# Top-32 attention and a gated MLP on one core: the first MLP layer on two token blocks at once

## The chip, the cores and the metric

The kernel runs on one core of a Trainium2 chip. The metric is the device time of one execution in microseconds. An execution of the kernel before takes 1560.32 us, the median of three runs.

## What is computed

Eight batches of eight heads are attended to, 576 tokens of 64 dimensions each. Of every row of scores only the 32 largest survive. The result goes through a two-layer MLP with a quick-GELU gate between.

```python
scores = (q @ k.T) / sqrt(64)                  # 8 batches, 8 heads, 576 x 576
kth    = 32nd largest of each row
p      = exp(where(scores >= kth, scores, -1e9) - rowmax)
attn   = (p / (p.sum(-1) + 1e-9)) @ v
x      = attn laid out as 4608 tokens x 512    # heads side by side
h      = x @ w_in                              # 512 -> 2048
g      = h / (1 + exp(-1.702 * h))
out    = g @ w_out                             # 2048 -> 512
```

All data are float32.

## The kernel before

**Slots and rounds.** The attention is cut into 144 slots, 18 for each batch. A slot is 128 query rows of one pair of heads. The first four full blocks of a batch (`t` = 0 to 3) have four slots each, one for each pair of heads. Two further slots hold the 64-row ends of two pairs of heads each, and they come between blocks 2 and 3. The first 12 slots are run one by one by `slot(n)`, with a plain search for the 32 largest, while the weights are loaded and rounded. All later ones are run two at a time by `two_slots(n)`, here called a round: 66 rounds find the largest of slots 12 to 143, and two more finish what is left. The order of the work within a round is written out by hand and holds for each engine's queue.

**What a round does.** In each half of a round, VectorE finds the largest of a slot (`topk_of_pairs`, begun by `pair_up`, line 322), GpSimd forms the lesser of each pair (lines 325 and 326), and ScalarE makes the exponentials (lines 387 and 390) and splits them (line 461) so that a DMA can transpose them by way of DRAM (lines 463 and 469). TensorE computes scores for two later slots (line 281), the attention output of two earlier slots (`values_at`, line 526), and two groups of each MLP layer. ScalarE copies scores out of PSUM (line 293).

**The MLP.** `x_of` (line 544, GpSimd) writes a slot's 128 columns of x into a tile `xT` of one block of 128 tokens. Where the last pair of heads of a block is in, `finish_x` puts the tile on the list `ready`. `hidden` (line 575) takes the first tile of the list and computes four of the sixteen slices of 128 hidden units, for the 128 tokens: 16 matmuls of 128 columns, which fill one PSUM bank. This is called a group here; a block has four. `tanh` (ScalarE, lines 592 and 595) and `gate` (GpSimd, lines 604 and 605; VectorE, line 607, at the end) turn the group into the gated activation, and `project` (line 622) multiplies it with `w_out`, four matmuls of 512 columns, into a PSUM bank `po` that collects the sixteen slices of a block. After the fourth group `leave` copies `po` out (line 628) and stores it. The 64-row ends of two batches make one further block of 128 tokens in a tile of their own (`xT_t`). That makes 36 blocks and 144 groups.

**Where a group can be computed.** A round calls `hidden` twice, once before the attention output of the round and once behind `x_of`, and `project` twice. Where `ready` is empty, the call does nothing. After the last round `last_slot` is repeated until all groups are done.

**Buffers.** There are two tiles `xT` (`xtp`), so the first `x_of` of a block waits until the groups of the block before the last are computed. In the rounds, the first `hidden` of a round writes into the bank `ps_h` and the second into the two-bank pool `ps_t`. Tiles for raw q and k (`loads`) are double, those for v (`vals`) sixfold. The tables READY, FETCH and VALUES say, for the four pairs of heads of a batch, how many slots before or after the batch's first slot they are prepared, loaded, and their v is loaded; READY_1 and FETCH_1 are those of the second batch.

Of the kernel before, what the change touches and what calls it, by code (L numbers as in the profile page):

```python
# [9 lines left out]
ALU = mybir.AluOpType  # L10
# [20 lines left out]
def kernel(  # L31
# [57 lines left out]
    const = ctx.enter_context(tc.tile_pool(name="const", bufs=1))  # L89
    pool = lambda name, bufs, **kw: ctx.enter_context(tc.tile_pool(name=name, bufs=bufs, **kw))  # L90
    raws = pool("raws", 8)
    loads = pool("loads", 2)
    vals = pool("vals", 6)
    qkt = pool("qkt", 6)
    scp = pool("scp", 4)
    prp = pool("prp", 2)
    lefts = pool("lefts", 2)
    small = pool("small", 4)
    ptp = pool("ptp", 2)
    xtp = pool("xtp", 2)  # L100
    xtt = pool("xtt", 1)
    thp = pool("thp", 5)
    apart = pool("apart", 4, space=DRAM)
# [54 lines left out]

    qT, kT, vv = {}, {}, {}
    loaded = {}  # L160
    v_ends = [const.tile([P, 2, D], F32, name=f"v_e{i}") for i in range(6)]
    for i, t in enumerate(v_ends):
        (nc.gpsimd if i else nc.vector).memset(t[:], 0.0)

# [6 lines left out]
    def load(name, b, hp, queue=None):  # L171

        src = q if name == "q" else k
        if (b, hp) not in loaded:
            loaded[b, hp] = loads.tile([P, 2 * NF + 1, 2, D], F32, name="qk_l")
        t = loaded[b, hp]
        if queue is None:
            heads_of = lambda j: of_load(name, t)[:, :, j, :]
        else:
            heads_of = lambda j: heads_apart(name, t)[:, j, :, :]  # L180
        queue = queue or nc.sync
        for j in range(2):
            queue.dma_start(heads_of(j), src[b, 2 * hp + j, 0:FULL, :].rearrange("(p t) d -> p t d", t=NF))

        on = slice(0, TAIL) if name == "q" else slice(TAIL, P)
        queue.dma_start(t[on, 2 * NF, :, :], src[b, 2 * hp : 2 * hp + 2, FULL:S, :].rearrange("h p d -> p h d"))
# [283 lines left out]

    xts = {}

    def values(n, put_off=None):

        b, t, hps = slots[n]
        pt = st[n]["pt"]
        outs = []
        for p in range(2 if t == NF else 1):
            cols = slice(p * TAIL, (p + 1) * TAIL) if t == NF else slice(0, P)
            main, tail = vv[b, hps[p]]  # L480
            o = ps_t.tile([P, 512], F32, name="o", tag="tp")
            for c in range(NF + 1):
                for j in range(2):
                    nc.tensor.matmul(
                        o[j * D : (j + 1) * D, 0 : cols.stop - cols.start],
                        lhsT=main[:, j, c, :] if c < NF else tail[:, j, :],
                        rhs=pt[:, MAIN[j] + c if c < NF else NF, cols],
                        start=(c == 0),
                        stop=(c == NF),
                    )  # L490
            outs.append((o, hps[p]))
        st[n].clear()

        def bring():
            for o, hp in outs:
                if t < NF:
                    if (b, t) not in xts:
                        xts[b, t] = xtp.tile([P, CC, P], F32, name="xT")
                    nc.scalar.copy(out=xts[b, t][:, hp, :], in_=o[:, 0:P])
                else:  # L500
                    if (b // 2, t) not in xts:
                        xts[b // 2, t] = xtt.tile([P, CC, P], F32, name="xT_t")
                    at = b % 2 * TAIL
                    nc.scalar.copy(out=xts[b // 2, t][:, hp, at : at + TAIL], in_=o[:, 0:TAIL])
            finish_x(n)

        if put_off is None:
            bring()
        else:
            put_off.append(bring)  # L510
# [24 lines left out]
    def x_of(m, o, by):  # L535

        b, t, hps = slots[m]
        for p in range(2 if t == NF else 1):
            cols = slice(p * TAIL, (p + 1) * TAIL) if t == NF else slice(0, P)
            key, tile_of = ((b // 2, t), xtt) if t == NF else ((b, t), xtp)  # L540
            if key not in xts:
                xts[key] = tile_of.tile([P, CC, P], F32, name="xT_t" if t == NF else "xT")
            to = slice(b % 2 * TAIL, (b % 2 + 1) * TAIL) if t == NF else cols
            nc.gpsimd.tensor_tensor(  # L544
                out=xts[key][:, hps[p], to], in0=o[:, cols], in1=by[:, cols], op=ALU.mult
            )
        finish_x(m)

    def finish_x(m):

        b, t, hps = slots[m]
        if hps[-1] == NP - 1:
            if t < NF:
                to = out[b * S : b * S + FULL, :].rearrange("(p t) c -> p t c", t=NF)[:, t, :]
                ready.append((xts.pop((b, t)), [(slice(0, P), to)]))
            elif b % 2:
                first = [(b - 1 + i) * S + FULL for i in range(2)]
                rows = [(slice(i * TAIL, (i + 1) * TAIL), out[x : x + TAIL, :]) for i, x in enumerate(first)]
                ready.append((xts.pop((b // 2, t)), rows))

    ready = []
    hidden_at = {"g": 0}
    to_gate, gated, to_project = [], [], []
    proj = {}

    def hidden(into=None):
        if not ready:
            return
        xT, rows = ready[0]
        g = hidden_at["g"]  # L570
        ph = (into or ps_h).tile([P, G, P], F32, name="ph", tag="tp" if into else "ph")
        for i in range(G):
            f = g * G + i
            for c in range(CC):
                nc.tensor.matmul(  # L575
                    ph[:, i, :],
                    lhsT=win[:, c, f * P : (f + 1) * P],
                    rhs=xT[:, c, :],
                    start=(c == 0),
                    stop=(c == CC - 1),  # L580
                )
        to_gate.append((ph, g, rows))
        hidden_at["g"] = (g + 1) % NG
        if g == NG - 1:
            ready.pop(0)

    def tanh(aside):

        if to_gate:
            ph, g, rows = to_gate.pop(0)  # L590
            th = thp.tile([P, G, P], F32, name="th")
            nc.scalar.activation(th[:], ph[:], AF.Tanh, scale=0.851 / RAISE)  # L592
            if aside:
                h = raws.tile([P, G, P], F32, name="h", tag="raw")
                nc.scalar.copy(out=h[:], in_=ph[:])
                ph = h
            gated.append((th, ph, g, rows))

    def gate(aside):
        if not gated:  # L600
            return
        th, h, g, rows = gated.pop(0)
        if aside:
            nc.gpsimd.tensor_scalar(th[:], th[:], 1.0, 1.0, op0=ALU.add, op1=ALU.mult)
            nc.gpsimd.tensor_tensor(out=th[:], in0=th[:], in1=h[:], op=ALU.mult)  # L605
        else:
            nc.vector.scalar_tensor_tensor(  # L607
                out=th[:], in0=th[:], scalar=1.0, in1=h[:], op0=ALU.add, op1=ALU.mult
            )
        to_project.append((th, g, rows))  # L610

    def project(blocks, put_off_leaving=False):

        if blocks[0] == 0:
            proj["on"] = to_project.pop(0)
            if proj["on"][1] == 0:
                proj["po"] = ps_p.tile([P, C], F32, name="po")
        gT, g, rows = proj["on"]
        po = proj["po"]
        for i in blocks:  # L620
            f = g * G + i
            nc.tensor.matmul(  # L622
                po[:], lhsT=gT[:, i, :], rhs=wout[:, f, :], start=(f == 0), stop=(f == FC - 1)
            )
        if blocks[-1] == G - 1 and g == NG - 1:
            def leave():
                ob = thp.tile([P, C], F32, name="ob", tag="th")
                nc.scalar.mul(out=ob[:], in_=po[:], mul=0.5 / RAISE**2)
                for on, to in rows:
                    nc.sync.dma_start(to, ob[on, :])  # L630

            leaving.append(leave)
            if not put_off_leaving:
                leave_all()

# [13 lines left out]


    READY = (-12, -10, -4, -2)
    READY_1 = (-6, -4, -3, -2)
    FETCH = (-16, -14, -8, -6)
    FETCH_1 = (-12, -10, -5, -3)
    VALUES = (-2, -1, 1, 2)
    by_slot = dict(enumerate([2, 2, 3, 3, 3, 3, 3, 3, 3, 3, 2, 2]))
    for n in by_slot:
        first = sum(map(len, list(by_slot.values())[:n]))
# [21 lines left out]

    def may_project(waiting):

        return len(to_project) > waiting and len(finished) >= NG * CC + (to_project[0][1] + 1) * G

    def both_heads(to, src, t):

# [67 lines left out]
    def slot(n):  # L754
# [65 lines left out]
            for fn, args in preparing:  # L820
                fn(*args)
        if n > PROJECTS and may_project(2):
            project(range(G))
        if idle:
            stay_warm(8)
        hidden()
# [1 line left out]
    def last_slot():  # L828

        tanh(False)  # L830
        gate(False)
        if may_project(0):
            project(range(G))
        hidden()

    def two_slots(n):

# [21 lines left out]

        def project_one():  # L860
            if may_project(0):
                project(range(G), True)

        def measure(m):
            if live(m):
# [7 lines left out]
            split(n - 1)  # L873
        bring_all()
        find(n)
        hidden()
        project_one()
        tanh(aside)
        prepare_some(first)
# [76 lines left out]
```

## Time and profile before

| | us |
|---|---|
| median of three runs | 1560.32 |
| lowest and highest | 1559.6 and 1564.83 |
| the profiled execution | 1561.79 |
| its span, first to last instruction | 1560.0 |

The profile shows one execution on the chip. TensorE is busy 94% of the span and VectorE 88%; the mean granted clock of TensorE is 0.972 of full speed. A float32 matmul of the program stands as two records in the trace, so a group of the first layer is 32 records of 128 columns and a group of the second 8 records of 512.

### The profile page before, as it was taken

To read this page: it belongs to the slowest core of one execution; us is meant where nothing else is said; L and a number is where in the kernel's file an instruction comes from. 1 tells how busy PE (TensorE), PEld (TensorE's weight loads), DVE (VectorE), ACT (ScalarE), POOL (GpSimd) and SP (SyncE) were. 2 spreads that over 40 slices of the span, in tenths; PEclk is the share of its full clock that TensorE was granted. 3 is DMA by queue.
4 is the path that set the end of the run, shared out by engine and by line. 5 is a ranking of instruction groups with operands and counts; after the bars stand their busy time and mean duration, and the time that the engine had idled before them with its cause. 6 is when DMAs were issued, how large, how long until landed. Compare 5 with 4: busy or idle time off the path is not lost. (4 is left out here: it accounts for less than half of the span.)

```text
span 1560.0 us, 31382 instructions
## 1 busy us (share of the span) xinstructions
PE 1461.0 (94%) x10729; PEld 1059.6 (68%) x10729; DVE 1375.2 (88%) x4542; ACT 1171.5 (75%) x1846; POOL 888.9 (57%) x1119
## 2 busy tenths in 40 slices
PE   7789789999999899999998899999998899999997
PEld 5667556777766577777776577777775677777765
DVE  7999989999989799999997799999997889999700
ACT  6998778888768687878786687888876688777710
POOL 3788555666645566666665466666664566666400
PEclk8899899999999999999999999999999999999999
DMA  7451786767755486677767576676765658444500
GB/s 241 134 160 36 194 214 184 194 172 183 189 156 162 126 199 173 173 176 181 187 162 161 128 186 190 163 189 175 179 172 146 161 147 203 131 128 130 145 23 14
DMA packets 533778, 248.35 MB, mean 159 GB/s; under 512 B 465136, under 2 KB 507889, under 8 KB 533617
## 3 DMA queue, kind: packets, MB, share of 16 engines
q1 hardware_dynamic: 533184, 246.05, 60.3%
q8 instruction: 84, 1.38, 0.4%
q14 instruction: 78, 0.63, 0.1%
q10 hardware_dynamic: 432, 0.30, 0.1%
HBM read 45.09 MB, written 105.32 MB: 96 GB/s over the span
## 5 line engine op out<-in xcount | busy, mean ns | idle before, releaser
L622 PE MATMUL po<-wout,th 128*128 128x512 f32 x1152 | 534.2, 608 | 43.9 <-POOL th L605 35.4
L575 PEld LDWEIGHTS ph<-xT,win 128*128 128x128 f32 x4096 | 473.9, 192 | 69.6 <-issue 53.2
L575 PE MATMUL ph<-xT,win 128*128 128x128 f32 x4096 | 489.3, 277 | 12.3 <-POOL xT L544 12.3
L622 PEld LDWEIGHTS po<-wout,th 128*128 128x128 f32 x1152 | 213.5, 195 | 264.5 <-issue 216.4
L336 DVE MAX8 top<-left 128x8 f32<-128x288 f32 x792 | 325.3, 445 | 0.0
L461 ACT COPY sc<-pr 128x2304 uint16<-128x2304 uint16 x133 | 281.5, 2117 | 2.2
L293 ACT ACTIVATE sc<-s_ps 128x576 f32<-128x576 f32 x288 | 172.2, 654 | 140.6 <-PE s_ps L281 130.3
L544 POOL TENSOR_TENSOR xT<-x 128x128 f32<-128x128 f32 x117 | 51.7, 458 | 392.6 <-DVE top L343 215.1
L390 ACT ACTIVATE pr<-sc,low 128x576 f32<-128x576 f32 x288 | 220.6, 774 | 47.7 <-POOL low L367 47.7
L336 DVE MAX8 top<-lesser 128x8 f32<-128x288 f32 x528 | 214.1, 446 | 37.1 <-POOL lesser L326 37.1
L339 DVE MATCH_REPLACE8 left<-top,left 128x288 f32<-128x288 f32 x528 | 229.6, 442 | 0.0
L387 ACT ACTIVATE sc<-sc,cut 128x576 f32<-128x576 f32 x288 | 208.7, 783 | 2.7 <-POOL cut L378 2.1
L326 POOL TENSOR_TENSOR lesser<-lesser,greater 128x576 int32<-128x576 int32 x132 | 186.0, 1409 | 22.7 <-DVE greater L322 13.2
L325 POOL TENSOR_TENSOR lesser<-sc 128x576 int32<-128x576 int32 x132 | 187.6, 1421 | 0.0
L281 PE MATMUL s_ps<-qk_t 64*128 64x288 f32 (+1 forms) x1280 | 185.2, 436 | 1.0 <-ACT sc L293 0.8
L605 POOL TENSOR_TENSOR th<-th,h 128x512 f32<-128x512 f32 x127 | 161.9, 1275 | 10.6
L526 PE MATMUL o<-pt,v_l 128*64 128x128 f32 (+1 forms) x2384 | 147.5, 268 | 11.0 <-DMA pt<-rows 11.0
L526 PEld LDWEIGHTS o<-pt,v_l 128*64 128x64 f32 x2384 | 122.7, 139 | 38.1 <-issue 22.9
L592 ACT ACTIVATE th<-ph 128x512 f32<-128x512 f32 x144 | 86.6, 602 | 81.0 <-PE ph L575 80.9
L322 DVE TENSOR_TENSOR greater<-sc 128x576 f32<-128x576 f32 x132 | 104.6, 792 | 44.7 <-ACT sc L293 35.4
L281 PEld LDWEIGHTS s_ps<-qk_t 64*128 64x128 f32 (+1 forms) x1280 | 100.8, 180 | 42.6 <-issue 22.1
L339 DVE MATCH_REPLACE8 left<-top,greater 128x288 f32<-128x288 f32 x264 | 114.8, 442 | 0.0
(86 smaller groups left out, 1606.2 us busy)
## 6 DMA issues: line engine op xcount, KB each, us to landing
rows<-sc SPq DMA_DIRECT2D x133, 576.0 KB, 3.1
qk_rows<-halves SPq DMA_DIRECT2D x56, 256.0 KB, 2.8
qk_l<-in_q_dram SPq DMA_DIRECT2D x64, 128.0 KB, 3.0
raw<-in_moe_w_in_dram SPq DMA_DIRECT2D x16, 512.0 KB, 5.2
v_l<-in_v_dram SPq DMA_DIRECT2D x32, 256.0 KB, 3.2
raw<-in_moe_w_out_dram SPq DMA_DIRECT2D x16, 512.0 KB, 3.6
out_dram<-ob SPq DMA_DIRECT2D x32, 256.0 KB, 2.9
qk_l<-in_k_dram SPq DMA_DIRECT2D x62, 128.0 KB, 2.9
```

The source lines that it names most:

```text
L281: nc.tensor.matmul(ps[i][rows, c, 0:HALF], lhsT=qT[b, hps[p]][on, cols], rhs=kT[b, hps[p]][on, FIRST[i] + c * HALF : FIRST[i] + (c + 1) * ...
L293: nc.scalar.mul(out=to, in_=ps[i][:, :, 0:HALF], mul=SCALE)
L325: nc.gpsimd.tensor_tensor(out=whole, in0=a.bitcast(I32), in1=b.bitcast(I32), op=ALU.add)
L326: nc.gpsimd.tensor_tensor(out=whole, in0=whole, in1=greater[n][:].bitcast(I32), op=ALU.subtract)
L336: nc.vector.max(top[:, i, 8 * r : 8 * r + 8], src[:, i, :])
L339: nc.vector.match_replace(to[:, i, :], top[:, i, 8 * r : 8 * r + 8], src[:, i, :], LOWEST)
L387: nc.scalar.activation(sc[:, i, :], sc[:, i, :], AF.Prelu, bias=cut[:, i : i + 1], alpha=HUGE)
L390: nc.scalar.activation(pr[:, i * S : (i + 1) * S], sc[:, i, :], AF.Exp, bias=low[:, i : i + 1], accum_out=den[:, i : i + 1],)
L461: nc.scalar.copy(out=halves, in_=pr[:].bitcast(U16).rearrange("p (k h) -> p h k", h=2))
L526: nc.tensor.matmul(o[j * D : (j + 1) * D, cols], lhsT=main[:, j, c, :] if c < NF else tail[:, j, :], rhs=pt[:, MAIN[j] + c if c < NF else ...
L575: nc.tensor.matmul(ph[:, i, :], lhsT=win[:, c, f * P : (f + 1) * P], rhs=xT[:, c, :], start=(c == 0), stop=(c == CC - 1),)
L622: nc.tensor.matmul(po[:], lhsT=gT[:, i, :], rhs=wout[:, f, :], start=(f == 0), stop=(f == FC - 1))
```

## The change

A block pair replaces the block in the first layer. From the third block of the first batch on, the tile `xT` holds two blocks (`x_at` finds the place in it), it goes on the list `ready` when the second of them is finished, and a matmul of `hidden` has 256 columns. A group is then two slices of hidden units for 256 tokens, and still fills one PSUM bank; a block pair has eight groups. `project` has two accumulators for a block pair, one in `ps_p` and one in `ps_h`, and the number of its matmuls in a group stays four. In the rounds and in `last_slot`, every `hidden` writes into `ps_t`. Blocks 0 and 1 of the first batch and the blocks of ends stay single.

`xtp` has three tiles, each of two blocks. To make room there is one tile for raw q and k and four for v; the first batch's second and fourth pairs of heads use the tiles of `ptp` as load buffers. The tables of loads move to fit. `last_slot` calls `hidden` ahead of `gate` and `project`.

```diff
-    loads = pool("loads", 2)
-    vals = pool("vals", 6)
+    loads = pool("loads", 1)
+    vals = pool("vals", 4)
-    xtp = pool("xtp", 2)
+    xtp = pool("xtp", 3)
...
-            loaded[b, hp] = loads.tile([P, 2 * NF + 1, 2, D], F32, name="qk_l")
+            home, tag = (ptp, "pt") if b == 0 and hp % 2 else (loads, "qk_l")
+            loaded[b, hp] = home.tile([P, 2 * NF + 1, 2, D], F32, name="qk_l", tag=tag)
...
+    def x_at(b, t, hp):
+        if t < NF:
+            if (b, t // 2) not in xts:
+                xts[b, t // 2] = xtp.tile([P, CC, 2, P], F32, name="xT")
+            return xts[b, t // 2][:, hp, t % 2, :]
+        if b // 2 not in xts:
+            xts[b // 2] = xtt.tile([P, CC, P], F32, name="xT_t")
+        return xts[b // 2][:, hp, b % 2 * TAIL : (b % 2 + 1) * TAIL]
...
     def finish_x(m):
...
+        if b == 0 and t < 2:
+            ready.append(([xT[:, c, t, :] for c in range(CC)], [rows(t)]))
+        elif t % 2:
+            ready.append(([xT[:, c, :, :].rearrange("p w q -> p (w q)") for c in range(CC)], [rows(t - 1), rows(t)]))
...
     def hidden(into=None):
...
+        tiles = len(rows)
+        f0 = hidden_at["f"]
+        fs = range(f0, f0 + G // tiles)
+        ph = (into or ps_h).tile([P, G * P], F32, name="ph", tag="tp" if into else "ph")
+        for i, f in enumerate(fs):
             for c in range(CC):
                 nc.tensor.matmul(
-                    ph[:, i, :],
+                    ph[:, i * tiles * P : (i + 1) * tiles * P],
                     lhsT=win[:, c, f * P : (f + 1) * P],
-                    rhs=xT[:, c, :],
+                    rhs=xT[c],
...
+    def project(put_off_leaving=False):
+        gT, fs, rows = to_project.pop(0)
+        if fs.start == 0:
+            pos[:] = [
+                home.tile([P, C], F32, name="po", tag=tag) for home, tag in ((ps_p, "po"), (ps_h, "ph"))[: len(rows)]
+            ]
+        blocks = iter(range(G))
+        for f in fs:
+            for po in pos:
+                i = next(blocks)
+                nc.tensor.matmul(
+                    po[:], lhsT=gT[:, i * P : (i + 1) * P], rhs=wout[:, f, :], start=(f == 0), stop=(f == FC - 1)
+                )
...
-    READY_1 = (-6, -4, -3, -2)
-    FETCH = (-16, -14, -8, -6)
-    FETCH_1 = (-12, -10, -5, -3)
-    VALUES = (-2, -1, 1, 2)
+    READY_1 = (-7, -4, -3, -2)
+    FETCH = (-16, -11, -8, -3)
+    FETCH_1 = (-12, -6, -3, -2)
+    VALUES = (-1, 1, 1, 3)
...
     def last_slot():
         tanh(False)
+        hidden(ps_t)
         gate(False)
         if may_project(0):
-            project(range(G))
-        hidden()
+            project()
...
         find(n)
-        hidden()
+        hidden(ps_t)
         project_one()
```

## Rows read from the trace of the kernel before

**Rows 1.** The page's first part: engine, busy us, share of the span, instructions.

```profile
PE 1461.0 (94%) x10729; PEld 1059.6 (68%) x10729; DVE 1375.2 (88%) x4542; ACT 1171.5 (75%) x1846; POOL 888.9 (57%) x1119
```

**Rows 2.** Stretches: start:end, length, engines' busy us (instructions), granted clock, DMA share, GB/s.

```profile
145.68:241.72 96.04, 80.28 (x536) 53.34 (x532) 90.90 (x309) 75.89 (x112) 52.05 (x65) 0.91 0.72 185
460.59:525.18 64.59, 52.95 (x368) 36.56 (x368) 46.02 (x160) 37.73 (x58) 34.50 (x44) 0.89 0.50 134
825.42:890.31 64.89, 53.24 (x368) 36.61 (x368) 46.03 (x160) 37.73 (x58) 34.50 (x44) 0.89 0.55 143
1190.55:1255.51 64.96, 53.31 (x368) 36.60 (x368) 46.02 (x159) 37.73 (x58) 34.48 (x44) 0.89 0.55 139
1106.89:1164.21 57.32, 57.32 (x416) 41.79 (x415) 56.09 (x193) 44.30 (x71) 36.27 (x46) 1.00 0.73 178
1505.84:1560.00 54.16, 43.23 (x216) 28.53 (x215) 4.12 (x6) 4.78 (x8) 0.00 (x0) 0.99 0.04 10
```

**Rows 3.** The chain that ended last, one round: start, us, engine, line.

```profile
1121.10 0.22 PE o L515 x2
1121.32 1.17 PE s_ps L281 x8
1122.49 2.33 PE o L526 x40
1124.83 1.17 PE s_ps L281 x8
1126.00 3.77 PE ph L575 x32
1129.77 3.44 PE po L622 x8
1133.20 3.57 PE ph L575 x32
1136.77 3.44 PE po L622 x8
1140.21 0.22 PE o L515 x2
```

**Rows 4.** VectorE's order of time, the first instruction of three slots [idle before].

```profile
1123.82 0.76 DVE L322 TENSOR_TENSOR greater<-sc 128x576 f32<-128x576 f32 x1
1133.15 0.76 DVE L322 TENSOR_TENSOR greater<-sc 128x576 f32<-128x576 f32 x1
1142.92 0.76 DVE L322 TENSOR_TENSOR greater<-sc 128x576 f32<-128x576 f32 x1 [0.17 <-ACT sc L293]
```

**Rows 5.** Waits of the span: who for whom, us in total, times, longest.

```profile
POOL xT L544 <- PE ph L575: 55.4, 6, 9.2
DVE top L336 <- POOL lesser L326: 37.1, 6, 6.2
PE ph L575 <- POOL xT L544: 12.3, 16, 1.1
```

**Rows 6.** Order of time in one stall (1190 to 1200 us).

```profile
1190.36 3.73 PE L575 MATMUL ph<-xT,win 128*128 128x128 f32 x32
1194.17 0.45 POOL L544 TENSOR_TENSOR xT<-x 128x128 f32<-128x128 f32 x1 [9.22 <-PE ph L575]
1197.48 0.82 DVE L336 MAX8 top<-lesser 128x8 f32<-128x288 f32 x2 [6.18 <-POOL lesser L326]
```

**Rows 7.** Stretches: a wait of TensorE in the round of slots 18 and 19, and after.

```profile
217.00:224.98 7.98, 2.01 (x29) 1.33 (x25) 6.39 (x22) 4.03 (x8) 0.00 (x0) 0.76 0.71 223
224.98:227.50 2.52, 2.52 (x22) 2.19 (x24) 2.52 (x11) 0.07 (x1) 0.00 (x0) 0.50 0.02 6
```

**Rows 8.** The chain after the last round, one repetition and the last matmuls.

```profile
1512.71 3.58 PE ph L575 x32
1516.32 0.61 ACT th L592
1516.95 0.70 DVE th L607
1517.69 3.70 PE po L622 x8
...
1552.41 3.71 PE po L622 x8
```

**Rows 9.** Waits of the DMA queue (SP): who for whom, us in total, times, longest.

```profile
SPq L469 <- DMA rows<-sc: 292.8, 106, 4.5
SPq L469 <- PE s_ps L281: 145.1, 53, 7.0
```

More of the change, by code (lines that the diff above doesn't have):

```diff
@@ L160 @@
     loaded = {}
-    v_ends = [const.tile([P, 2, D], F32, name=f"v_e{i}") for i in range(6)]
+    v_ends = [const.tile([P, 2, D], F32, name=f"v_e{i}") for i in range(NP)]
     for i, t in enumerate(v_ends):
@@ L495, in bring @@
             for o, hp in outs:
[L496 to L504, printed above, removed]
+                to = x_at(b, t, hp)
+                nc.scalar.copy(out=to, in_=o[:, 0 : to.shape[-1]])
             finish_x(n)
@@ L539, in x_of @@
             cols = slice(p * TAIL, (p + 1) * TAIL) if t == NF else slice(0, P)
[L540 to L546, printed above, removed]
+            nc.gpsimd.tensor_tensor(out=x_at(b, t, hps[p]), in0=o[:, cols], in1=by[:, cols], op=ALU.mult)
         finish_x(m)
@@ L551, in finish_x @@
         b, t, hps = slots[m]
[L552 to L556, printed above, removed]
+        if hps[-1] < NP - 1:
+            return
+        if t == NF:
+            if b % 2:
                 first = [(b - 1 + i) * S + FULL for i in range(2)]
                 rows = [(slice(i * TAIL, (i + 1) * TAIL), out[x : x + TAIL, :]) for i, x in enumerate(first)]
-                ready.append((xts.pop((b // 2, t)), rows))
+                xT = xts.pop(b // 2)
+                ready.append(([xT[:, c, :] for c in range(CC)], [rows]))
+            return
+        lines = out[b * S : b * S + FULL, :].rearrange("(p t) c -> p t c", t=NF)
+        rows = lambda t: [(slice(0, P), lines[:, t, :])]
+        xT = xts[b, t // 2]
+        if b == 0 and t < 2:
+            ready.append(([xT[:, c, t, :] for c in range(CC)], [rows(t)]))
+        elif t % 2:
+            ready.append(([xT[:, c, :, :].rearrange("p w q -> p (w q)") for c in range(CC)], [rows(t - 1), rows(t)]))
+        if t % 2:
+            del xts[b, t // 2]
     ready = []
-    hidden_at = {"g": 0}
+    hidden_at = {"f": 0}
     to_gate, gated, to_project = [], [], []
-    proj = {}
+    pos = []
     def hidden(into=None):
@@ L569, in hidden @@
         xT, rows = ready[0]
[L570 to L573, printed above, removed]
+        tiles = len(rows)
[3 more added lines that the diff above has]
+        for i, f in enumerate(fs):
             for c in range(CC):
                 nc.tensor.matmul(
-                    ph[:, i, :],
+                    ph[:, i * tiles * P : (i + 1) * tiles * P],
                     lhsT=win[:, c, f * P : (f + 1) * P],
-                    rhs=xT[:, c, :],
+                    rhs=xT[c],
                     start=(c == 0),
@@ L581, in hidden @@
                 )
-        to_gate.append((ph, g, rows))
-        hidden_at["g"] = (g + 1) % NG
-        if g == NG - 1:
+        to_gate.append((ph, fs, rows))
+        hidden_at["f"] = fs.stop % FC
+        if fs.stop == FC:
             ready.pop(0)
@@ L590, in tanh @@
             ph, g, rows = to_gate.pop(0)
-            th = thp.tile([P, G, P], F32, name="th")
+            th = thp.tile([P, G * P], F32, name="th")
             nc.scalar.activation(th[:], ph[:], AF.Tanh, scale=0.851 / RAISE)
             if aside:
-                h = raws.tile([P, G, P], F32, name="h", tag="raw")
+                h = raws.tile([P, G * P], F32, name="h", tag="raw")
                 nc.scalar.copy(out=h[:], in_=ph[:])
@@ L610, in gate, with leave @@
         to_project.append((th, g, rows))
[L612 to L626, printed above, removed]
+    def project(put_off_leaving=False):
[11 more added lines that the diff above has]
+                )
+        if fs.stop == FC:
+            def leave(po, to_rows):
                 ob = thp.tile([P, C], F32, name="ob", tag="th")
                 nc.scalar.mul(out=ob[:], in_=po[:], mul=0.5 / RAISE**2)
-                for on, to in rows:
+                for on, to in to_rows:
                     nc.sync.dma_start(to, ob[on, :])
-            leaving.append(leave)
+            leaving.extend(lambda po=po, to=to: leave(po, to) for po, to in zip(pos, rows))
             if not put_off_leaving:
@@ L681, in may_project @@
     def may_project(waiting):
-        return len(to_project) > waiting and len(finished) >= NG * CC + (to_project[0][1] + 1) * G
+        return len(to_project) > waiting and len(finished) >= NG * CC + to_project[0][1].stop
     def both_heads(to, src, t):
@@ L830, in last_slot @@
         tanh(False)
+        hidden(ps_t)
         gate(False)
         if may_project(0):
-            project(range(G))
-        hidden()
+            project()
     def two_slots(n):
@@ L861, in project_one @@
             if may_project(0):
-                project(range(G), True)
+                project(True)
         def measure(m):
```

## The prediction

> **What bounds the kernel now.** I read the engines' shares first. TensorE is busy 94% of the span and VectorE 88% [rows 1], so neither alone explains 1560 us, and the stages have to be taken apart. The next view is the table of stretches [rows 2]. In an undisturbed one, three rounds from 1106.89 to 1164.21, TensorE is busy all 57.32 us and VectorE 56.09. The chain shows one such round [rows 3]: from 1121.10 to 1140.21 is 19.11 us, and TensorE's pieces lie end to end in it, scores 2.34, attention output 2.33, two groups of the first layer 7.34, two of the second 6.88, the row sums 0.22. TensorE sets the round. VectorE is close behind: its first instruction of a slot comes after 9.33 and 9.77 us in turn, 0.17 of it waiting [rows 4], so that it would need 9.33 + 9.60 = 18.93 us by itself.
>
> The undisturbed round does not explain the span either. Three stretches of five slots took 64.59, 64.89 and 64.96 us [rows 2]; five slots at 9.555 (half of 19.11) are 47.78. So 194.44 − 143.33 = 51.1 us are lost there, in six stalls. The list of waits names them: GpSimd's write into `xT` waited six times for the first layer's matmuls, 55.4 us, and behind it VectorE waited six times 6.2 us for the lesser half [rows 5]. In one of them [rows 6] the fourth group ends at about 1194.1 and the write starts at 1194.17, after 9.22 us; what GpSimd owes VectorE is queued behind it, and VectorE goes on at 1197.48. The code gives the reason. The blocks of ends push their four groups between blocks 2 and 3 of every second batch; `hidden` then runs four groups late, and with two `xT` tiles the next two blocks each find their tile still being read.
>
> The third place is the end. Behind the last round each repetition is first layer 3.58, tanh 0.61, gate 0.70, second layer 3.70 [rows 8]; TensorE is idle between the two, some 1.4 us.
>
> **The change part by part.** The sum is made against the profiled execution, 1561.79 us (span 1560.0, 1.8 around it), which is 1.5 us above the median.
>
> (a) Three tiles of two blocks. I followed the list `ready` through the slots. The first write into the k-th tile must find the groups of tile k − 3 done. Batch 2's second pair is first written in round 46, and its tile was last read in round 36; batch 3's first in round 56, last read in round 48. This gap of four rounds or more repeats, so all six stalls go: −51.1 us. What is late next is TensorE, with the round of 19.11 us. Both ends of this term are near: the loss is measured against undisturbed rounds of the same trace.
>
> (b) 256 columns. A record of 128 columns costs 3.57 / 32 = 111.6 ns in a stream, one of 512 costs 3.44 / 8 = 430 ns [rows 3]. The trace has none of 256. On the line between the two it is 217.7 ns, and a group of 16 of them 3.48 us, 0.09 less. At the rate of 512 columns it would be 215 ns and 3.44 us (0.13 less); with no gain a column, 3.57 (0). I take the line. By the list there are 15 block pairs, 120 wide groups, 112 of them in rounds: −10.1 us, ends −14.6 and 0. The round falls to 19.11 − 0.18 = 18.93, which is just what VectorE needs, so the lower end is cut off at VectorE's pace and I use it for the range with half its excess. The loads of weights lie under the matmuls, and their halved number gains nothing more.
>
> (c) Groups that start on data just written. TensorE waited 16 times for `xT`, 12.3 us [rows 5]: a block becomes ready in the very half round in which its first group is called. With block pairs I count eight such starts, and in each TensorE first has the six records of the three chunks that are already there, 6 × 0.218 = 1.31 us where it was 6 × 0.112 = 0.67. So the mean wait, 12.3 / 16 = 0.77, falls by 0.64 to 0.13: −12.3 + 1.0 = −11.3 us, ends −12.3 and −4 (VectorE's pace swallows the rest).
>
> (d) The front. Blocks 2 and 3 of the first batch become ready together in round 20, where block 2 alone was ready in round 14. Four groups of each layer vanish from rounds 14 to 20. There VectorE is busy 90.90 of 96.04 us [rows 2], so at most 5.1 us can be gained by TensorE's relief; but part of what VectorE lacks is the wait for a transpose, for which TensorE stood with 2.01 us of work in 7.98 [rows 7], and that does not go. I take 0, ends −5 and +5.
>
> (e) The end. The last pair becomes ready after the last slot, so the four groups missing in front are done here. From 1505.84 TensorE then does 3.44, a single-block repetition of 3.57 + 3.44, eight of 3.48 + 3.44, and 3.44 again: 69.3 us, if `hidden` ahead of `project` covers tanh and gate (0.61 + 0.70 us [rows 8] under 3.44 of second layer). Now the same stretch is 54.16 [rows 2], the last matmul ends at 1552.41 + 3.71 = 1556.1 [rows 8], so 50.3 of it is the matmuls'. The term is +19.0 us, ends +18 and +27 (the upper: a gap of about 1.3 us remains six times). Two output copies at once add some 0.5 us at the very end.
>
> (f) Queues, PSUM and loads, at nothing. `hidden` in `ps_t` in both halves makes three takers in a round of two banks. Each bank is read out by tanh and its copy, and the next taker comes after a second-layer group (3.44 us) at the earliest, mostly after two. The second accumulator in `ps_h` finds the bank free, as no round uses it otherwise. With one load buffer and four v tiles, SP, whose queue is in order, waits for ScalarE's copy of raw q and k or for the attention output. But it waits there already: the transposes wait 53 times behind the scores and the attention output next to them, 145.1 us, and 106 times for rows [rows 9]. A v load asks for the attention output of the same half round, at most 1.2 us (half of 2.33) later, and the row writes queued behind it need ScalarE's exponentials, which come later still. If this cover is gone, see the second rival.
>
> A rule that speaks against (d). In the stretch to 224.98 TensorE worked 2.01 of 7.98 us, and right behind it the granted clock was 0.50, the 1.2 GHz level [rows 7]. The Trainium skill, "TensorE: Matmul & The Clock Gate", section "Why this matters for your kernels", asks that no idle gaps stand between bursts of matmuls, since the clock then falls to half. The trace agrees with it here, and by it the relieved front runs at half clock. What that would cost is the third rival.
>
> **The sum.** −51.1 − 10.1 − 11.3 + 0 + 19.0 + 0.5 = −52.9 us: 1561.8 − 52.9 = 1508.9, and 1507.4 on the scale of the median. TensorE and VectorE then need the same 18.93 us for a round, and two that are level seldom never wait; I round up, to 1508.
>
> **The rivals.**
>
> First, the round stays at 19.11. VectorE's 18.93 was read while GpSimd and ScalarE follow TensorE; if the chain of scores, copy and search sets the pace, (b) gives nothing and (c) half: 1508 + 10 + 6 = 1524. For it: VectorE is busy 56.09 of 57.32 us [rows 2]. Against it: its own wait is 0.17 us in a round and is for scores that TensorE delivers [rows 4]. Chance 0.14.
>
> Second, slower: SP's waits with one load buffer and single v tiles. At a batch boundary loads stand ahead of a slot's row write; if they hold it until the next half round, the transpose, the attention output behind it on TensorE and the scores behind that come late, and VectorE starves as in the stalls, about 51.1 / 6 = 8.5 us each time. Seven boundaries at 8.5 are 60 us: 1568. It decides from 52.9 / 7 = 7.6 us a boundary. Against it: (f). Chance 0.05.
>
> Third, the cold front. From round 16 to 20 TensorE has 2.34 + 2.33 + 0.22 = 4.9 us of work in a round [rows 3]. At 1.2 GHz this is 4.9 us longer, and it lies between transposes and scores. Four rounds with all of it on VectorE's path are 20 us: 1528. Against it: scores are computed two slots ahead. Chance 0.09.
>
> Fourth, the change doesn't do what it says: a tile is held for eight groups rather than four, and if I have the list wrong the waits for `xT` stay. Then 1508 + 51 = 1559. Chance 0.04.
>
> **How the numbers follow.** The forecast has 0.68. Its own range is 1500 (front −5, half the further gain of (b), −2, and −1 at (c)) to 1521 (front +5, (e) +8 at its end). The range of 1498 to 1527 takes 2 us more below, for terms that come together, takes in the first rival and leaves out the second and fourth and the most of the third. A measurement of this kernel tells about 0.3%, 4.7 us, from no change. Faster: 0.68 + 0.14 + 0.09 = 0.91. Same: 0.04, the fourth. Slower: 0.05.
>
> **What would show it.** Right: no wait of GpSimd's write into `xT` for the first layer's matmuls, and no stretch of five slots over 50 us; records of 256 columns about 217 ns apart; rounds of 18.9 us; behind the last round some 69 us of TensorE without gaps; a clock of 0.5 around rounds 16 to 20. Wrong: rounds still of 19.1 us (first rival), SP waits on loads followed by VectorE gaps at each batch boundary (second), gaps of VectorE of several us in rounds 16 to 20 (third).

## The result and the profile after

The changed kernel takes 1516.72 us (median of four runs, 1515.49 to 1517.86) beside 1561.67 for the kernel before in the same comparison: a ratio of 0.971, interval 0.969 to 0.973. It is 45 us faster; the forecast was 1508 with 1498 to 1527 around it. The profiled execution has a span of 1515.2 us, 44.8 less than before.

The first part of the page of the changed kernel answers to [rows 1]:

```profile
PE 1437.7 (95%) x8809; PEld 994.8 (66%) x8809; DVE 1382.2 (91%) x4546; ACT 1171.4 (77%) x1842; POOL 859.7 (57%) x1109
```

TensorE has 1920 records fewer and 23 us less to do. The gain is larger than that, so the rest came from waits. GpSimd's wait for the first layer's matmuls, the first line of [rows 5], is gone. These are its waits for `xT` now, and three others that matter below (changed kernel, waits of the span: who for whom, us in total, times, longest):

```profile
POOL xT L544 <- ACT x L912: 246.2, 54, 11.8
PE o L530 <- DMA pt<-rows: 17.7, 10, 7.2
ACT halves L240 <- DMA qk_l<-in_k_dram: 14.2, 3, 7.9
DVE greater L323 <- ACT sc L294: 6.3, 1, 6.3
```

One round in the chain of the changed kernel (start, us, engine, line), beside [rows 3]:

```profile
284.64 3.65 PE ph L584 x16
288.30 3.43 PE po L632 x8
291.73 3.45 PE ph L584 x16
295.18 3.43 PE po L632 x8
298.83 1.17 PE s_ps L282 x8
300.00 2.34 PE o L530 x40
302.34 1.17 PE s_ps L282 x8
303.51 3.65 PE ph L584 x16
```

The round is 303.51 − 284.64 = 18.87 us where it was 19.11. A wide group takes 3.45 us in a stream, 3.45 / 16 = 215.6 ns for a record of 256 columns.

To see where the 44.8 us are, take two marks that stand for the same work in both kernels: the first row sum of round 22 on TensorE (a round has the number of its first slot), and the second-layer group behind the last group but two of the last block of ends. In the kernel before (TensorE's order of time; then its chain):

```profile
253.64 0.38 PE L515 MATMUL o<-ident,wide 128*128 128x128 f32 x2
...
1505.84 6.87 PE po L622 x16
```

In the changed kernel:

```profile
259.78 0.38 PE L519 MATMUL o<-ident,wide 128*128 128x128 f32 x2
...
1441.87 3.44 PE po L632 x8
```

| stretch | before, us | after, us | difference | forecast |
|---|---|---|---|---|
| start to round 22 | 253.6 | 259.8 | +6.1 | 0 |
| round 22 to the end's first group | 1252.2 | 1182.1 | −70.1 | −72.5 |
| the end | 54.2 | 73.3 | +19.2 | +19.5 |
| sum | 1560.0 | 1515.2 | −44.8 | −53.0 |

The prediction's terms add up to −53.0; it wrote −52.9. Of the 8.2 us by which they were too low, 6.1 are in the front, where it had put nothing, and 2.4 in the rounds.

### The profile page after: what moved, and what is told of

Read it like the earlier page. It is cut to its first block, busy times and chain, and to the rows that moved or that the text cites. A ratio compares the mean times of both kernels' runs of the same rounds, so it can differ in the third digit from the quotient of the medians.

```text
span 1515.2 us, 27569 instructions
## 1 busy us (share of the span) xinstructions
PE 1437.7 (95%) x8809; PEld 994.8 (66%) x8809; DVE 1382.2 (91%) x4546; ACT 1171.4 (77%) x1842; POOL 859.7 (57%) x1109
## 4 chain that ended last, share of the span: by engine, by line
DVE 59%; PE 22%; issue 3%; DMA 2%; SPq 2%; ACT 1%; POOL 0%; DVEq 0%; ACTq 0%; POOLq 0%
DVE top L337 26%; DVE left L340 16%; PE ph L584 9%; PE po L632 9%; DVE lesser L340 6%; DVE greater L323 5%; DVE top L344 3%; PE o L530 2%; PE s_ps L282 2%; DVE cut L347 1%; DMA pt<-rows 1%; DMA rows<-sc 1%; SPq L470 1%; DVE inverse L423 1%; DVE sums L421 1%
## 5 line engine op out<-in xcount | busy, mean ns | idle before, releaser
L632 PE MATMUL po<-wout,th 128*128 128x512 f32 x1152 | 518.2, 593 | 1.5 <-POOL wout L147 1.5
L584 PE MATMUL ph<-xT,win 128*128 128x256 f32 (+1 forms) x2176 | 472.2, 370 | 1.2 <-POOL xT L544 0.7
L584 PEld LDWEIGHTS ph<-xT,win 128*128 128x128 f32 x2176 | 389.2, 190 | 101.5 <-issue 47.2
L632 PEld LDWEIGHTS po<-wout,th 128*128 128x128 f32 x1152 | 217.2, 190 | 217.2 <-issue 205.5
L544 POOL TENSOR_TENSOR xT<-x 128x128 f32<-128x128 f32 x117 | 56.1, 497 | 268.7 <-ACT x L912 246.2
L282 PE MATMUL s_ps<-qk_t 64*128 64x288 f32 (+1 forms) x1280 | 188.9, 442 | 10.4 <-ACT sc L294 7.8
L530 PE MATMUL o<-pt,v_l 128*64 128x128 f32 (+1 forms) x2384 | 150.1, 271 | 17.7 <-DMA pt<-rows 17.7
L614 POOL TENSOR_TENSOR th<-th,h 128x512 f32<-128x512 f32 x123 | 156.8, 1275 | 10.3
L368 POOL TENSOR_SCALAR low<-cut,top 128x1 f32<-128x1 f32 x264 | 66.8, 269 | 93.9 <-DVE cut L347 93.5
```

The costliest lines, as they stand in the source:

```text
L282: nc.tensor.matmul(ps[i][rows, c, 0:HALF], lhsT=qT[b, hps[p]][on, cols], rhs=kT[b, hps[p]][on, FIRST[i] + c * HALF : FIRST[i] + (c + 1) * ...
L530: nc.tensor.matmul(o[j * D : (j + 1) * D, cols], lhsT=main[:, j, c, :] if c < NF else tail[:, j, :], rhs=pt[:, MAIN[j] + c if c < NF else ...
L584: nc.tensor.matmul(ph[:, i * tiles * P : (i + 1) * tiles * P], lhsT=win[:, c, f * P : (f + 1) * P], rhs=xT[c], start=(c == 0), stop=(c == ...
L632: nc.tensor.matmul(po[:], lhsT=gT[:, i * P : (i + 1) * P], rhs=wout[:, f, :], start=(f == 0), stop=(f == FC - 1))
```

## The experiments

My theory: a third tile ends the six stalls; the wider matmul and fewer starts on fresh data give some 20 us; the four groups shifted to the end cost 27, of which the new order of the end gives back 8; the miss is the load buffer in front. The main rival: the pairs of blocks are what gains, and the tiles only make them possible. Each kernel below was timed beside the kernel before on one chip. From before to after there is a chain of three of them, each one step further.

**e1, the third tile alone.** The kernel before with three single tiles; room for it is made as in the change, at the v tiles.

```diff
-    vals = pool("vals", 6)
+    vals = pool("vals", 4)
-    xtp = pool("xtp", 2)
+    xtp = pool("xtp", 3)
-    VALUES = (-2, -1, 1, 2)
+    VALUES = (-1, 1, 1, 3)
```

> The kernel before with a third single-block tile xT; to make room v has four tiles, with the v table of the changed kernel. Everything else stays (two load buffers, matmuls of 128 columns, old end). Theory (the third tile alone ends the six stalls, 51.1 us, and the round stays at TensorE's 19.11): 1561.7 - 51 = 1511 us, no wait of GpSimd for the first layer's matmuls. Rival (the stalls go because pairs change when groups are ready, and a third single tile doesn't reach): 1545 or more.

Measured: 1510.68 us, ratio 0.968 (0.966 to 0.969), so 50 us less than before. In its waits GpSimd never waits for the first layer's matmuls; TensorE still waits for `xT` as in [rows 5] (waits of e1):

```profile
PE ph L575 <- POOL xT L544: 11.2, 15, 0.8
```

The rival falls: one more tile of 128 tokens gives nearly all that the stalls cost (51.1 us), and more than the whole change.

**e2, and the new end.** e1 with `hidden` ahead of `gate` in the last repetitions.

```diff
     def last_slot():
         tanh(False)
+        hidden(ps_t)
         gate(False)
         if may_project(0):
             project(range(G))
-        hidden()
```

> As the run with the third tile, and last_slot in the new order, with hidden into ps_t ahead of gate and project. Theory (five gaps of 1.41 us and five slow starts of 0.26 go): 8.3 us below that run, 1502 to 1503 us, and so 14 us below the changed kernel. Rival (tanh and gate stay on the path): as that run, 1511.

Measured: 1501.48 us, ratio 0.962 (0.960 to 0.964), 9.2 below e1. The end's chain of e2 has TensorE alone, where [rows 8] had tanh and gate between:

```profile
1463.97 3.57 PE ph L575 x32
1467.54 3.44 PE po L622 x8
1470.97 3.57 PE ph L575 x32
```

**e7, and one load buffer.** The changed kernel with single blocks: e2 with the changed kernel's load buffer and its tables READY_1, FETCH and FETCH_1 (as in the change's diff).

> The changed kernel with single blocks and matmuls of 128 columns: three single tiles, one load buffer, four v tiles, the new tables, the new end. Against e2_third_tile_new_end it has only the one load buffer and its tables. Theory (loads cost 3.5 us at the start and one VectorE gap of 6.3 us in front, pairs cost four groups at the end, 27.6 us, and give back some 0.1 us a round): 1507 to 1512 us, 5 to 10 below the changed kernel. Rival (pairs pay): above 1517 us.

Measured: 1509.62 us, ratio 0.967 (0.966 to 0.969). The one load buffer, with its tables, costs 8.1 us against e2. From e7 to the changed kernel only the pairs remain, and they cost 7.1 us.

**e3, the change with the old end.** The reverse of e2's edit, on the changed kernel.

```diff
     def last_slot():
         tanh(False)
-        hidden(ps_t)
         gate(False)
         if may_project(0):
             project()
+        hidden(ps_t)
```

> The changed kernel with last_slot in the old order, hidden behind project. Theory (nine repetitions have a gap of 1.41 us and a slow start of 0.26 again): 1516.7 + 15 = 1532 us. Rival (other work covers it): 1517.

Measured: 1529.69 us, ratio 0.981, so 13 us more than with the new end. TensorE's order of time in e3 shows the gap [idle before]. A repetition takes 1489.92 − 1481.36 = 8.56 us, where it is 3.45 + 3.43 = 6.88 in the changed kernel:

```profile
1481.36 3.70 PE L632 MATMUL po<-wout,th 128*128 128x512 f32 x8 [1.41 <-DVE th L616]
1484.89 3.62 PE L584 MATMUL ph<-xT,win 128*128 128x256 f32 x16
1489.92 3.70 PE L632 MATMUL po<-wout,th 128*128 128x512 f32 x8 [1.41 <-DVE th L616]
```

**e5, two double tiles.**

```diff
-    xtp = pool("xtp", 3)
+    xtp = pool("xtp", 2)
```

> The changed kernel with two tiles of two blocks instead of three. Theory (a pair's first write waits where the pair before the last is still being read; by the list this is so three times, in rounds 46, 82 and 118): three stalls of about 8.5 us, 1516.7 + 25 = 1542 us. Rival (two double tiles are enough, since they hold four blocks): 1517.

Measured, in a single run and so without an interval: 1541.19 us, 24.5 more than the changed kernel. The stalls are back, three as counted (waits of e5):

```profile
POOL xT L544 <- PE ph L584: 26.9, 3, 9.0
DVE top L337 <- POOL lesser L327: 15.1, 3, 6.0
```

**e6, less work for VectorE.** The trace after shows VectorE without one wait between 285 and 1386 us, and its merge stretched where GpSimd works at the same time. The chain that ended last, by engine, points the same way:

```profile
DVE 59%; PE 22%; issue 3%; DMA 2%; SPq 2%; ACT 1%; POOL 0%; DVEq 0%; ACTq 0%; POOLq 0%
```

So I took VectorE for the bound of the new round, and left the merge out.

```diff
-        return ops + [merge, bound]
+        return ops + [lambda: None, bound]
```

> The changed kernel without VectorE's merge (the elementwise maximum of two lists of 16 at the end of a slot's search), which is left out. It takes 1.07 us of VectorE in a round, 0.7 of it standing behind GpSimd. Theory (VectorE sets the round of 19.03 us, and TensorE with 18.86 is next): rounds of 18.86 to 18.9, 8 to 10 us less, 1507 to 1509 us. First rival (TensorE's work is not a bound at all): rounds of about 18, 1460 us. Second rival (VectorE doesn't set the round): 1517 us.

Measured: 1513.13 us, ratio 0.969 (0.967 to 0.971), 3.6 less than the changed kernel where 8 to 10 were expected, and the two intervals overlap. From slot 24 to slot 142 the mean round is 19.05 us beside 19.03. My theory falls. The stretch from 700 to 1000 us (length, busy us of the engines, granted clock, DMA share, GB/s), first in the changed kernel:

```profile
700.00:1000.00 300.00, 298.76 (x1842) 205.96 (x1841) 295.67 (x1009) 250.58 (x381) 181.53 (x241) 1.00 0.71 184
```

then in e6, with VectorE's waits from 285 to 1386 us under it:

```profile
700.00:1000.00 300.00, 299.02 (x1839) 205.89 (x1836) 280.41 (x979) 251.06 (x382) 190.61 (x243) 1.00 0.71 184
...
DVE greater L323 <- ACT sc L294: 62.6, 58, 1.9
```

VectorE does 15 us less in these 300, and as much time turns into waits for scores. TensorE is busy 299 of 300 in both, with as many records. TensorE sets the round, as before the change, and VectorE follows closely. Where two engines are nearly level, the chain doesn't tell which of them sets the time; taking work from one does.

**e8, data that come sooner.** e2 still has the waits of [rows 5] for fresh data. There, ScalarE's copy of the attention output stood behind the exponentials; e8 moves it between their two steps.

```diff
+        def bring_x():
+            if held:
+                x = raws.tile([P, 2, 2, P], F32, name="x", tag="raw")
...
         if live(n):
-            exponentials(n)
-        if held:
-            x = raws.tile([P, 2, 2, P], F32, name="x", tag="raw")
...
+            exponentials(n, bring_x)
+        else:
+            bring_x()
```

> As e2_third_tile_new_end, and in the second half of a round ScalarE's copy of the attention output and GpSimd's writes into xT stand between the two steps of the exponentials, where they stood behind both. In e2_third_tile_new_end 15 rounds take 20.1 us and the others 19.1; in the long ones the first layer's second group starts on a tile that GpSimd is still writing. Theory (that wait costs a whole 1.0 us of the round each time, and data that come 1.5 us sooner end it): 15 us less than e2_third_tile_new_end, 1486 us, all rounds of 19.1. Rival (VectorE or ScalarE needs those 20.1 us): 1501 us.

Measured: 1487.52 us, ratio 0.952 (0.951 to 0.954), 14 less than e2. TensorE's order of time in e2, from one row sum to the next, is a round of 20.11 us:

```profile
620.01 0.38 PE L515 MATMUL o<-ident,wide 128*128 128x128 f32 x2
625.00 0.94 PE L575 MATMUL ph<-xT,win 128*128 128x128 f32 x6
626.68 3.17 PE L575 MATMUL ph<-xT,win 128*128 128x128 f32 x26 [0.74 <-POOL xT L544]
633.12 3.73 PE L575 MATMUL ph<-xT,win 128*128 128x128 f32 x32
640.12 0.38 PE L515 MATMUL o<-ident,wide 128*128 128x128 f32 x2
```

The same round in e8 takes 19.11:

```profile
616.60 0.38 PE L515 MATMUL o<-ident,wide 128*128 128x128 f32 x2
621.59 3.84 PE L575 MATMUL ph<-xT,win 128*128 128x128 f32 x32
628.70 3.73 PE L575 MATMUL ph<-xT,win 128*128 128x128 f32 x32
635.71 0.38 PE L515 MATMUL o<-ident,wide 128*128 128x128 f32 x2
```

This is the fastest version found, with blocks of 128 tokens, 29 us below the changed kernel.

**e9, the change with its loads spaced.**

```diff
-    READY_1 = (-7, -4, -3, -2)
+    READY_1 = (-8, -6, -4, -2)
-    FETCH_1 = (-12, -6, -3, -2)
+    FETCH_1 = (-12, -7, -5, -3)
-            home, tag = (ptp, "pt") if b == 0 and hp % 2 else (loads, "qk_l")
+            home, tag = (ptp, "pt") if b == 0 and hp % 2 else (prp, "pr") if (b, hp) == (0, 2) else (loads, "qk_l")
```

> The changed kernel with its loads spaced: the second batch's raw q and k are fetched a half round or slot ahead of their preparation each time (FETCH_1 -12, -7, -5, -3 and READY_1 -8, -6, -4, -2), and the first batch's third pair is loaded into a buffer of the pool prp, so that it needn't wait for the first pair. Theory (the one load buffer costs 3.5 us at the start, where the third pair's load waits for the first pair's tile, and 6.3 us in round 16, where ScalarE stands before a load that was issued in the same half round): 7 to 10 us less, 1507 to 1510 us, no VectorE gap over 2 us in front. Rival (the front is long because TensorE runs at half clock there): 1515 us or more.

Measured: 1512.73 us, ratio 0.968 (0.966 to 0.970), 4.0 less than the changed kernel instead of 7 to 10, between the two theories. In the front it did what was expected: VectorE's first instruction of slot 22 comes at 238.83 us instead of 246.52, and its largest wait left in rounds 12 to 22 is 1.74 us. But only 4.5 us of the 7.7 are left in the span of the profiled execution. By TensorE's row sums e9 is 6.7 us ahead in round 22 and 4.5 at the end, and 1.8 of the difference lie in one round of 22.77 us, which takes 20.97 in the changed kernel. Its wait for a late transpose is hardly longer, 2.04 us beside 1.88. But right behind it the granted clock is lower, and two groups of matmuls take 1.6 us more (e9, order of time; then stretches with the granted clock as the third figure from the end):

```profile
1154.45 2.06 PE L282 MATMUL s_ps<-qk_t 64*128 64x288 f32 x8
1156.45 4.54 PE L584 MATMUL ph<-xT,win 128*128 128x256 f32 x16
...
1154.45:1156.45 2.00, 2.00 (x11) 1.00 (x9) 1.97 (x8) 1.88 (x2) 1.22 (x3) 0.57 0.85 245
1156.45:1161.00 4.55, 4.55 (x19) 3.94 (x18) 4.51 (x15) 1.81 (x3) 2.90 (x4) 0.81 1.01 193
```

In the changed kernel the same two groups take 1.24 and 3.72 us, at a granted clock of 1.00.

## Why the prediction was right, point by point

The direction, the size and the range held. The loads, (f), are the step that failed; the other steps came out near their numbers, some of them by errors that cancel. That the range takes in the cost of the loads is luck: its upper end was set for the first rival.

**(a) The tiles: right.** −51.1 forecast; e1 measured 50.2 for the third tile alone. e5 put three stalls back at 24.5 us, 8.2 each, at the count that the list `ready` gave. Behind slot 22 no five slots of the changed kernel take over 49.5 us; ahead of it they take up to 54.45, which belongs to (f).

**(b) The wide matmul: right, and the line between 128 and 512 columns was too careful.** 215.6 ns for a record, not 217.7: 0.12 us a group, 13.4 us for 112 groups where 10.1 were forecast. The upper bound, 215 ns, was nearer.

**(c) Fresh data: mechanism right, both sizes off.** A start on fresh data costs the kernel before a whole 1.0 us of its round, not the 0.77 that TensorE's wait shows: e8 gained 14 us for 15 such rounds. The wait itself is 0.74, and the records around it take 0.94 + 3.17 = 4.11 us where those of a group in e8 take 3.84. With pairs such a round takes 19.23 and not 18.87 us, 0.36 more where 0.13 was said. The two errors nearly cancel.

**(d) and (f) The front and the loads: (f) wrong, and this is the miss.** I had put the loads at nothing, because SP waits at the same places anyway. But it was not SP's queue that mattered; it was ScalarE's. With one buffer, the second batch's third and fourth pairs are fetched in the same half round in which ScalarE copies them, and ScalarE, in order, stands before that copy with everything behind it. The changed kernel in round 16 (order of time, idle before in brackets):

```profile
204.05 2.11 ACT L240 COPY halves<-qk_l 128x2304 uint16<-128x2304 uint16 x1 [5.33 <-DMA qk_l<-in_k_dram]
206.07 1.18 ACT L294 ACTIVATE sc<-s_ps 128x576 f32<-128x576 f32 x2
206.76 2.82 PE L282 MATMUL s_ps<-qk_t 64*128 64x288 f32 x8 [7.07 <-ACT sc L294]
207.35 0.76 DVE L323 TENSOR_TENSOR greater<-sc 128x576 f32<-128x576 f32 x1 [6.33 <-ACT sc L294]
```

Scores wait for ScalarE to empty their banks, and VectorE for the scores: 6.3 us. At the very start the third pair's load waits for the first pair's tile, which makes slot 12 begin at 149.22 us and not 145.68, 3.5 later. e7 measured 8.1 us for the load buffer with its tables, and e9 took the gap and the late start away (slot 12 begins at 145.17 us there). The wait of 6.3 us is not lost whole: slots 12 to 22 take 97.30 us where they took 96.04 [rows 2]. What the front lost by each part is read from the row sum of round 22 along the chain of experiments, from 253.64 us before to 259.78 in the changed kernel (e2, then e7, order of time):

```profile
251.14 0.38 PE L515 MATMUL o<-ident,wide 128*128 128x128 f32 x2
256.84 0.38 PE L516 MATMUL o<-ident,wide 128*128 128x128 f32 x2
```

So e2 is 2.5 us sooner than the kernel before, for a reason that was not traced; the load buffer costs 5.7; and the pairs cost 2.9, where (d) had taken 0 with 5 to either side. TensorE's relief gave nothing back. I had named what is queued behind the wait on SP and not what is queued behind the next one on ScalarE.

**(e) The end: right.** +19.2 against +19.5, without gaps; e3 shows what the old order would have cost, 13 us (15 expected).

**The rivals.** The first (the round stays at 19.11) did not come about, but the round's mean, 19.03 us between slots 24 and 142, lies above the 18.93 that I took: the plain wide rounds have 18.87, those with single groups 19.10, the starts on fresh data 19.23, and five rounds have up to 2.1 us more, 5.9 together. The latter are the second rival at a small price: TensorE waits for a transpose behind a batch's loads, 4.7 us between 285 and 1440 us and not 60 (the rest of the 17.7 above lies in the front, where VectorE sets the time). In the third, the cold front, the clock did fall: 0.75 between slots 12 and 22 instead of 0.91 [rows 2].

```profile
149.22:246.52 97.30, 56.65 (x358) 35.23 (x356) 88.58 (x309) 71.28 (x103) 43.45 (x57) 0.75 0.75 185
```

TensorE is idle over 40 of these 97 us, as it was to be with four groups gone. VectorE lost next to nothing by the clock there: its waits are the 6.3 us above, which a load made, and 1.5. With the loads spaced (e9) the same slots take no longer at 0.75 than in e2 at 0.91 (e9, then e2):

```profile
145.17:238.83 93.66, 57.35 (x343) 35.19 (x343) 90.09 (x310) 68.30 (x100) 44.37 (x57) 0.75 0.72 179
145.25:239.01 93.76, 80.17 (x526) 53.08 (x524) 90.31 (x310) 74.93 (x109) 52.01 (x65) 0.91 0.73 187
```

The Trainium skill's "TensorE: Matmul & The Clock Gate", section "Why this matters for your kernels", has the rule that idle gaps between bursts of matmuls bring the clock down. It holds here for the clock itself and did not decide the time. Whether the clock is why TensorE's round 22 comes 2.9 us later with the pairs is not shown.

**And the change as a whole.** It gains 45 us, and its parts pull in opposite directions: e1 has 50 for the tile, e2 adds 9 for the end, e7 loses 8 for the load buffer, and the pairs, which the change is named after, lose 7. Where they lose is read from the two marks of the table above, since e7 differs from the changed kernel by the pairs alone. The first mark of e7 is the 256.84 us above; the second is this (chain):

```profile
1463.69 3.44 PE po L623 x8
```

With its span of 1509.5 us, e7's three stretches are 256.8, 1206.9 and 45.8 us. So the pairs cost 2.9 us in the front, gain 24.8 in the rounds and cost 27.5 at the end: a loss of 5.7 between the two profiled executions, and e7's was 1.7 above its median. The gain is what 13.4 us of matmuls and some 12 of fresh data (15 rounds at 1.0 less 8 at 0.36) add up to; the loss at the end is the groups that come too late for the front and are done alone. Rounds that a late transpose makes longer stand in both kernels (e7's longest takes 23.57 us) and don't tell them apart. The forecast had the terms to see this: −10.1, −11.3, and for the end +19.0 with the new order's saving in it, which is some +27 without the 8 that this order saves with single blocks too. It did not add them up by themselves; the sum of +6 would have said that the pairs lose.

## What to carry to other kernels

Where an engine waits for a buffer, count when each buffer is written and last read, and add one of the size that is there, before anything is made larger. A coarser unit of work is ready later: what it takes from the front comes back at the end, where nothing else runs beside it, so price both ends before the rate in the middle. And follow a wait through every queue in order: the transfer that was late stopped ScalarE, which was nowhere near its limit at 77%.

## What the runs showed of the hardware

VectorE's merge, two inputs of 32 values a partition, takes between 191 and 1453 ns in the changed kernel with a median of 194. It is long where it meets a GpSimd operation that reads SBUF. Of the 132 merges 60 take over 250 ns; each of them begins while GpSimd is at work, and ends 47 to 60 ns behind the end of that operation. Of the 72 short ones 69 begin with no GpSimd operation under way. One of the long ones (changed kernel, order of time, GpSimd and then VectorE):

```profile
1048.22 1.40 POOL L326 TENSOR_TENSOR lesser<-sc 128x576 int32<-128x576 int32 x1
```

```profile
1048.74 0.94 DVE L344 TENSOR_TENSOR top<-top 128x32 f32<-128x32 f32 x1
```

It ends at 1049.68, just behind GpSimd's end at 1049.62. The Trainium skill, "SBUF — State Buffer", section "SBUF: two separate sides", says that the two engines share a pair of ports that one of them holds for a whole instruction; this is what the rows look like. So VectorE's busy time in a profile holds waiting, and I had read it as need: e6 took the merge away and the round stayed.
